# Phase roundings on either engine, half of the filter tables copied in SBUF, split projections in the first batch, and a new written order

## The chip, the cores and the metric

The kernel runs on one core of a Trainium2 chip. A core has five engines that work at the same time, each through its own instructions in order: TensorE for matmuls (PE; its weight loads are listed apart as PEld), VectorE (DVE), ScalarE (ACT), GpSimd (POOL) and SyncE (SP), which here only starts DMA transfers. POOL starts DMA transfers too. They meet through semaphores. Matmuls write PSUM, which has eight banks; DVE and ACT read PSUM, POOL in this kernel works on SBUF alone.

The metric is the device time of one execution in microseconds (us), the median of the runs shown. A "span" is the time from the first to the last instruction of the one profiled execution.

## The reference

Eight batches. First an attention with a feature map in place of a softmax over the sequence, then a gate with a long convolution done by Fourier transforms along the sequence:

```python
def phi(x):
    proj = np.einsum('bhsd,df->bhsf', x, w_phi)
    proj = proj - np.max(np.abs(proj), axis=-1, keepdims=True)
    return np.concatenate([np.exp(proj), np.exp(-proj)], axis=-1)
q_p, k_p = (phi(q), phi(k))
kv = np.einsum('bhsf,bhsd->bhfd', k_p, v)
z = np.sum(k_p, axis=2)
num = np.einsum('bhsf,bhfd->bhsd', q_p, kv)
den = np.einsum('bhsf,bhf->bhs', q_p, z)[..., None] + 1e-06
x = num / den          # then (B, S, H * D)
proj = x @ w_proj
x1, x2, x3 = (proj[..., :D], proj[..., D:2 * D], proj[..., 2 * D:])
X2 = np.fft.rfft(x2, n=S, axis=1)
H = np.fft.rfft(filter_fft, n=S, axis=0)[None, :, :]
x2_conv = np.fft.irfft(X2 * H, n=S, axis=1)
y = x1 * x2_conv * x3
return (y @ w_out).astype(np.float32)
```

Batch 8, heads 8, sequence S = 576, head dimension 64, 128 features, model width D = 512. Inputs and output are float32; the kernel computes in bf16 with float32 sums.

## The kernel before, in words

**An order written out by hand.** The whole program is one string, `PLAN` (lines 28 to 188), of some 1450 words. A word is the name of a method and its arguments; `@n` gives the first PSUM bank that it uses. `run` (L1036) goes through the words and calls each method once, so every engine gets its instructions in the order of the words that use it. Nothing reorders them afterwards. A word such as `Oe,ACT,3,1` or `Oe,DVE,3,1` names the engine that does the step.

**Per batch**, in the names of the words:

- `load` and `loadh` start the transfer of q, k or v (whole, or half the heads) on POOL's queue, with a cast to bf16. `trh` turns q and k by a DMA transpose on SP's queue; for batch 0 PE does this instead (`pt`), and `pte` copies the result from PSUM (into the tiles `qT`, `kT`).
- `Qn` and `Pk` project on PE; `maxq` and `maxk` take the absolute maxima on DVE (L695). `mhi`, `mlo`, `trm`, `trme` bring q's maxima into rows. `Pq` projects q again and subtracts the maxima, all on PE.
- `ex` takes the exponentials on ACT (L681), 16 per batch with both signs, `exkt` and `exqt` those of the last ninth of the sequence. `em` takes exponentials of k's maxima, and `vs` scales v by them (L742): four calls per batch, one for each sign and half.
- `KV` sums over the sequence on PE, `KVe` copies it out. `NE` multiplies by q's exponentials, `rc` and `xn` (L785, L790) divide; `xn,b,v` gives a quarter of the attention output of batch b. `trx` transposes it by DMA into `xT`, in batch 0 `ptx` on PE with `ptxe`. `NEt`, `rct`, `xnt` do the rest of the sequence.
- `f1`, `f2` (L839, L845) fold the output, `F` transforms it on PE, `Fe` and `Fet` copy it out. `X2` projects in the frequency domain, `Y1` (L878, L883) multiplies by the filter's tables, `m3` (L887) adds. `X1` and `X3` project in time through `proj` (L889): eight matmuls of 256 columns, two directions `d` times four row blocks `kt`. `X1e` copies x1 out and `tm` multiplies it by x3.
- `I` transforms back, `Ie`, `Ip`, `Im`, `ym` put halves and the gate together (in the last batch `J` and `yj`), `O` projects out, `Oe` copies, `st` stores on SP's queue.

**The start, once per run.** The cosine and sine tables (`D`, `Dt`, `inv`) are computed on the chip. POOL writes index patterns (`gen_rows`: tiles `fr` and `nr`), DVE writes columns of factors (`gen_cols`: `cols`). A phase is a pattern times a factor; it is rounded to a whole number by writing it as int16 (tile `whole`, L444 and L449) and the remainder (tile `turn`, L438) is what the Sin on ACT takes (`gen_sin`, L459). Both steps stand in `gen_angles` (L433) on DVE. There are nine roundings: two each in `gen_angles,0` and `gen_angles,2`, two in `gen_angles,3` and three in `gen_angles,4`. `D1m` and `D1e` build a mirrored table of `D`. `filt_load` brings the filter in eight transfers on SP's queue, `filt_loadt` its rest; `filt_fold` (L511) adds and subtracts its halves, `H` transforms it on PE, and `H_ev` (L538, L540) writes the tables `HTe`, `HTo` and `H5` from PSUM, with scale factors that are numbers or columns 16 to 18 of `cols`. It reads PSUM nine times.

**The `port` rule.** `run` calls `port` (L1022) after each word. For words in the list `PORT`, when done by DVE, it remembers the DVE instruction; the next POOL step of that list (or a pattern step) gets a dependence on it. So POOL is held until that DVE step is done; there is no such hold the other way.

**Buffers** are rings of tiles (`RING`, `at`), two to six deep; `late` closes the scratch tiles of the start and opens those of the gate.

Of the kernel before, what the change touches and what calls it, by code (L numbers as in the profile page):

```python
# [24 lines left out]
PORT = ("f1", "f2", "m3", "vs", "ym", "mlo", "filt_fold", "gen_ends", "gen_five")  # L25
# [4 lines left out]
gen_part w_load,phi gen_rows,1 gen_cols,0 loadh,q,0,1 filt_load,3 gen_ident gen_cols,1 filt_load,1  # L30
loadh,q,0,0 gen_rows,0 filt_loadt loadh,k,0,0 gen_angles,4 loadh,k,0,1 filt_load,2 load,q,1
w_load,proj,0 pt,q,0,0,0@0 pt,q,0,0,1@1 gen_one gen_sin,4 w_phi filt_load,0 gen_angles,2
w_load,proj,1 load,v,0 gen_angles,3 gen_sin,2 load,k,1 pt,k,0,1,0@2 pt,q,0,1,1@3 gen_angles,0
pt,q,0,1,0@4 gen_neg pt,k,0,1,1@5 pt,k,0,0,1@6 gen_sin,3 pte,DVE,q,0,0,1@1 gen_back gen_sin,0
pte,DVE,q,0,0,0@0 pte,DVE,q,0,1,1@3 Qn,0,0@0 filt_fold,POOL,2 pte,DVE,k,0,1,0@2 pte,ACT,k,0,1,1@5
pt,k,0,0,0@7 trh,q,1,0 pte,DVE,q,0,1,0@4 D1m@2 pte,ACT,k,0,0,1@6 maxq,0,0@0 Qn,0,1@4
pte,ACT,k,0,0,0@7 filt_fold,POOL,1 D1e,ACT@2 Pk,0,1@6 maxq,0,1@4 Pkt,0@0 Qnt,0@2 maxqt,0@2 Pk,0,2@4
trh,q,1,1 filt_fold,POOL,0 maxkt,0@0 ex,k,p,0,2@4 Qn,0,3@2 maxq,0,3@2 exkt,p,0@0 exkt,m,0@0
maxk,0,1@6 ex,k,m,0,2@4 Pk,0,0@2 Qn,0,2@0 load,q,2 ex,k,p,0,0@2 maxq,0,2@0 ex,k,m,0,0@2 maxk,0,2@4
Pk,0,3@0 mhi,0 ex,k,p,0,3@0 zeros H,0@4 maxk,0,0@2 mlo,POOL,0 gen_five,POOL ex,k,m,0,3@0 trm,0@5  # L40
ex,k,m,0,1@6 H,2@2 maxk,0,3@0 H,3@3 ex,k,p,0,1@6 trme,DVE,0@5 H_ev,DVE,0@4 Pq,0,2@0 trh,k,1,0
em,p,0,0 em,m,0,0 H,1@7 vs,POOL,p,0,0 em,p,0,1 H_ev,ACT,3@3 H_ev,DVE,2@2 Pq,0,1@4 H_ev,DVE,1@7 H,4@6
ex,q,p,0,2@0 vs,POOL,m,0,0 ex,q,m,0,2@0 Qn,1,1@2 late trh,k,1,1 H_ev,DVE,4@6 em,m,0,1 ex,q,m,0,1@4
Pq,0,0@0 maxq,1,1@2 Qn,1,0@6 ex,q,p,0,1@4 vs,POOL,m,0,1 maxq,1,0@6 Qnt,1@2 ex,q,m,0,0@0 KV,0,0@4
maxqt,1@2 ex,q,p,0,0@0 vs,POOL,p,0,1 Qn,1,2@6 Pqt,0@2 maxq,1,2@6 KVe,ACT,0,0@4 Qn,1,3@0 trh,q,2,0
exqt,p,0@2 NE,0,0@4 exqt,m,0@2 maxq,1,3@0 Pq,0,3@6 gen_ends,POOL KV,0,1@2 ex,q,m,0,3@6 trh,q,2,1
rc,0,0@4 xn,0,0@4 NE,0,1@0 mhi,1 w_load,out KVe,ACT,0,1@2 mlo,DVE,1 ptx,0,0@4 rc,0,1@0 load,v,1
NE,0,2@2 ptxe,ACT,0,0@4 xn,0,1@0 ex,q,p,0,3@6 rc,0,2@2 f1,POOL,0,0,0 Pkt,1@0 xn,0,2@2 NEt,0@4
maxkt,1@0 NE,0,3@6 f1,POOL,0,0,1 rct,0@4 ptx,0,2@2 exkt,p,1@0 ptx,0,1@3 rc,0,3@6 xn,0,3@6 exkt,m,1@0
f2,POOL,0,0,0 xnt,0,0@4 ptxe,ACT,0,1@3 ptx,0,3@6 ptxe,DVE,0,2@2 trm,1@7 Pk,1,1@0 xnt,0,1@4  # L50
ptxe,ACT,0,3@6 Pk,1,0@2 f1,POOL,0,1,1 maxk,1,1@0 trme,ACT,1@7 ptxt,0@4 ex,k,p,1,0@2 Qn,2,0@5
X1,0,0@7 w_load,proj,2 f1,DVE,0,1,0 ex,k,m,1,0@2 ptxte,DVE,0@4 maxq,2,0@5 f2,POOL,0,1,1 X1,0,2@4
ex,k,m,1,1@0 maxk,1,0@2 f2,POOL,0,1,0 X1t,0@5 X1e,ACT,0,0@7 ex,k,p,1,1@0 Qn,2,2@6 X1te,DVE,0@5
f2,POOL,0,0,1 F,0,2@2 maxq,2,2@6 X1e,ACT,0,2@4 Qn,2,3@0 em,m,1,0 load,k,3 Fet,ACT,0,2@2 F,0,3@4
Fe,ACT,0,2@2 maxq,2,3@0 F,0,0@6 load,k,2 Fet,ACT,0,3@4 Fe,ACT,0,3@4 Qn,2,1@2 Fe,ACT,0,0@6
vs,POOL,m,1,0 Pk,1,3@0 maxq,2,1@2 Qnt,2@4 Fet,ACT,0,0@6 ex,k,m,1,3@0 F,0,1@6 maxqt,2@4 X1,0,1@2
ex,k,p,1,3@0 Fe,DVE,0,1@6 load,q,3 Pq,1,0@4 Fet,DVE,0,1@6 em,p,1,0 maxk,1,3@0 X1e,ACT,0,1@2 Pk,1,2@6
vs,POOL,p,1,0 ex,q,m,1,0@4 X2,0,3@3 maxk,1,2@6 X2,0,2@0 ex,q,p,1,0@4 trh,k,3,1 X2,0,1@1 Y1,0,3@3
em,p,1,1 em,m,1,1 vs,POOL,p,1,1 ex,k,p,1,2@6 X2,0,0@4 Y1,0,2@0 ex,k,m,1,2@6 Pq,1,1@2 Y1,0,0@4
X2,0,4@5 ex,q,m,1,1@2 vs,POOL,m,1,1 trh,k,2,0 KV,1,0@6 mhi,2 Y1,0,4@5 ex,q,p,1,1@2 Y1,0,1@1 Pq,1,2@4  # L60
# [18 lines left out]
trx,2,1 Pqt,2@4 Pq,2,3@6 KVe,ACT,2,1@0 trh,q,4,0 NE,2,0@2 exqt,m,2@4 X2,1,0@0 exqt,p,2@4 rc,2,0@2
xn,2,0@2 ex,q,m,2,3@6 Pq,2,2@4 Y1,1,0@0 f1,POOL,2,0,1 X2,1,1@3 ex,q,p,2,2@4 X2,1,3@2 f1,POOL,2,0,0  # L80
ex,q,m,2,2@4 Y1,1,1@3 trh,q,4,1 X3t,1@0 ex,q,p,2,3@6 f2,POOL,2,0,1 X2,1,4@1 Y1,1,3@2 trh,k,4,0
X1t,1@3 m3,DVE,1,0 Pk,3,1@6 X1te,ACT,1@3 NE,2,2@4 Y1,1,4@1 trx,2,0 ex,k,m,3,1@6 m3,POOL,1,1 NE,2,3@2
rc,2,2@4 O,0,1@1 xn,2,2@4 ex,k,p,3,1@6 rc,2,3@2 trx,2,2 xn,2,3@2 O,0,2@4 Oe,ACT,0,1@1 tmt,1@0
# [107 lines left out]
class Kernel:  # L191
# [901 lines left out]
```

## Time and profile before

| | |
|---|---|
| three runs | 306.33, 313.06, 305.88 us |
| median | 306.33 us |
| the profiled execution | 307.0 us |
| its span | 305.2 us |
| mean granted TensorE clock in it | 0.982 |
| memory read and written in it | 33.75 MB and 9.44 MB |

How to read what follows. The page gives busy time per engine as a share of the span and of the instructions counted; then strips of 40 equal slices, 7.63 us each, in which a digit is the busy share in tenths (9 is 90% or more) and PEclk the granted clock in tenths. The chain of waits goes back from the last instruction through what released each step. Rows of groups have the line, engine and operation, what is written and read, the count, the busy time and the mean in ns of one, and then the idle time just ahead of them with what ended it. Rows of the timeline begin with the start and the length in us. Ends of neighbouring instructions on one engine overlap a little, so the distance from start to start is some 0.1 us shorter than the length.

### The profile page before, as it was taken

The page shows a single profiled execution, that of the slowest core. Times are in us where ns is not written, and L with a number is a line of the kernel's source. Part 1 is how long each engine was busy: PE and PEld are TensorE (multiplying, and loading weights), DVE is VectorE, ACT ScalarE, POOL GpSimd, SP SyncE. Part 2 cuts the span into 40 slices and gives each one's busy share as a digit, 9 for nine tenths or more (in the row PEclk, how much of TensorE's full clock was granted, in tenths as well). Part 3 has the DMA queues.
Part 4 walks back from the last instruction along what each step waited for, and adds up shares of the span by engine and source line. Part 5 has one row for each costly group of instructions (what it writes and reads, how often), then busy time and mean ns, then how long its engine had stood idle before and what let it go on. Part 6 is the DMA issues. An engine that isn't in the chain of part 4 may idle for free.

```text
span 305.2 us, 10169 instructions
## 1 busy us (share of the span) xinstructions
PE 270.7 (89%) x4259; PEld 198.1 (65%) x4289; DVE 258.9 (85%) x444; ACT 218.3 (72%) x370; POOL 227.4 (74%) x199
## 2 busy tenths in 40 slices
PE   0184898998999989999999999999999999999990
PEld 0162486586777668586767778667677857986750
DVE  8768999987987998989998898988899988776940
ACT  3649979984998869987784988788977596631121
POOL 9662899979994898998995995999669855782200
PEclk9996999999999999999999999999999999999997
DMA  6999979996999969996697548697901660361357
GB/s 121 222 206 173 192 120 186 164 170 93 163 177 146 134 138 184 194 150 128 116 180 111 114 60 128 141 166 131 168 5 21 128 142 2 53 133 33 66 127 155
DMA packets 71902, 39.98 MB, mean 131 GB/s; under 512 B 52208, under 2 KB 66672, under 8 KB 71856
## 3 DMA queue, kind: packets, MB, share of 16 engines
q1 hardware_dynamic: 57040, 23.08, 44.8%
q0 software_dynamic: 14816, 16.25, 34.2%
q8 instruction: 33, 0.54, 0.8%
q14 instruction: 13, 0.11, 0.1%
HBM read 33.75 MB, written 9.44 MB: 141 GB/s over the span
## 4 chain that ended last, share of the span: by engine, by line
PE 74%; DVE 11%; DMA 5%; issue 3%; ACT 3%; POOL 2%; SPq 0%; DVEq 0%; POOLq 0%; ACTq 0%
PE ps L895 16%; PE ps L873 11%; PE ps L1007 9%; PE ps L757 6%; PE ps L948 5%; PE ps L771 5%; DVE mq L695 4%; DMA kn<-in_k_dram 3%; PE ps L653 3%; DVE mk L695 2%; PE ps L904 2%; PE ps L851 2%; PE ps L659 2%; PE ps L619 2%; PE ps L855 2%
## 5 line engine op out<-in xcount | busy, mean ns | idle before, releaser
L895 PE MATMUL ps<-xT,wproj 128*128 128x256 bf16 x512 | 65.1, 273 | 1.2 <-DMA xT<-xn 0.8
L895 PEld LDWEIGHTS <-wproj 128*128 128x128 bf16 x512 | 47.5, 98 | 10.5 <-issue 1.9
L695 DVE TENSOR_REDUCE mq<-ps 128x8 f32<-128x1024 f32 (+1 forms) x40 | 43.8, 1112 | 6.0 <-PE ps L626 3.3
L695 DVE TENSOR_REDUCE mk<-ps 128x8 f32<-128x1024 f32 (+1 forms) x40 | 44.2, 1109 | 1.5 <-ACT Ekm L681 1.0
L839 POOL TENSOR_TENSOR SD<-xn 128x512 bf16<-128x512 bf16 x30 | 34.1, 1153 | 12.4 <-DVE xn L790 8.3
L742 POOL TENSOR_TENSOR vp<-vn,vp 128x1152 bf16<-128x1152 bf16 x16 | 34.4, 2152 | 10.3 <-ACT vp L736 8.9
L742 POOL TENSOR_TENSOR vm<-vn,vm 128x1152 bf16<-128x1152 bf16 x15 | 32.2, 2152 | 8.6 <-DVE T L887 6.3
L681 ACT ACTIVATE Eqm<-ps 128x1024 bf16<-128x1024 f32 x32 | 32.7, 1030 | 6.7 <-PE ps L659 5.7
L996 POOL TENSOR_TENSOR yT<-cv,x1s 128x576 bf16<-128x576 f32 x27 | 34.0, 1279 | 4.5 <-DVE cv L955 3.1
L845 POOL TENSOR_TENSOR xf<-SD 128x512 bf16<-128x512 bf16 x32 | 36.5, 1154 | 1.1
L1007 PE MATMUL ps<-wout,yT 128*128 128x512 bf16 x129 | 33.8, 379 | 1.3 <-issue 0.6
L681 ACT ACTIVATE Ekp<-ps 128x1024 bf16<-128x1024 f32 x32 | 33.1, 1035 | 2.1 <-DVE mk L695 1.9
L681 ACT ACTIVATE Eqp<-ps 128x1024 bf16<-128x1024 f32 x32 | 32.9, 1029 | 2.3 <-PE ps L659 2.2
L681 ACT ACTIVATE Ekm<-ps 128x1024 bf16<-128x1024 f32 x32 | 32.8, 1036 | 2.2 <-PE ps L619 1.4
L873 PE MATMUL ps<-wproj,XF 128*128 128x512 bf16 x116 | 30.0, 379 | 0.7 <-issue 0.2
L284 ACT CAST x1s<-ps 128x512 bf16<-128x512 f32 (+1 forms) x31 | 16.7, 548 | 17.5 <-PE ps L904 12.3
L887 POOL TENSOR_TENSOR T<-T,T 128x1024 bf16<-128x1024 bf16 x10 | 21.2, 2126 | 9.3 <-DVE T L883 8.4
L284 ACT COPY o<-ps 128x512 f32<-128x512 f32 x28 | 16.4, 591 | 12.6 <-PE ps L1007 11.6
L955 DVE TENSOR_TENSOR cv<-es,ps 128x288 f32<-128x288 f32 x56 | 22.4, 446 | 2.1 <-ACT es L952 1.9
L948 PE MATMUL ps<-inv,T 128*128 128x288 bf16 x168 | 23.8, 286 | 0.1
L790 DVE TENSOR_TENSOR xn<-ps,r 128x512 bf16<-128x512 f32 x32 | 22.1, 691 | 1.3
L883 DVE TENSOR_TENSOR T<-ps,HTe 128x1024 bf16<-128x1024 f32 x16 | 19.3, 1220 | 4.4 <-PE ps L873 4.4
(169 smaller groups left out, 654.0 us busy)
## 6 DMA issues: line engine op xcount, KB each, us to landing
out_dram<-o SPq DMA_DIRECT2D x72, 128.0 KB, 2.4
vn<-in_v_dram POOLq DMA_DIRECT2D x8, 576.0 KB, 8.5
qn<-in_q_dram POOLq DMA_DIRECT2D x7, 576.0 KB, 9.0
kn<-in_k_dram POOLq DMA_DIRECT2D x7, 576.0 KB, 6.8
wproj<-in_moe_w_proj_dram POOLq DMA_DIRECT2D x3, 512.0 KB, 13.8
fl<-in_moe_filter_fft_dram SPq DMA_DIRECT2D x8, 128.0 KB, 7.1
qn<-in_q_dram POOLq DMA_DIRECT2D x2, 288.0 KB, 7.2
kn<-in_k_dram POOLq DMA_DIRECT2D x2, 288.0 KB, 9.7
```

The costliest lines, as they stand in the source:

```text
L284: self.nc.scalar.copy(dst, src)
L681: self.nc.scalar.activation(e, p, AF.Exp, bias=0.0, scale=1.0 if g == "p" else -1.0)
L695: self.nc.vector.tensor_reduce(out=out, in_=src, axis=AX.X, op=ALU.max, apply_absolute_value=True)
L742: self.eng(eng).tensor_tensor(out=t[:, :, :, 0:64], in0=self.at("vn", b)[:, 2 * X:2 * X + 2], in1=t[:, :, :, 64:65].to_broadcast([128, 2, ...
L839: self.eng(eng).tensor_tensor(out=o[:, :, 2 * i:2 * i + 2, :], in0=x[:, :, 0:2, :], in1=x[:, :, 2:4, :], op=ALU.subtract if i else ALU.add)
L845: self.eng(eng).tensor_tensor(out=o[:, :, 2 * i:2 * i + 2, :], in0=x[:, :, 0:4:2, :], in1=x[:, :, 1:4:2, :], op=ALU.subtract if i else ALU ...
L873: self.mm(self.pb(0), l, w[:, kt, 512:1024], start=(kt == 0), stop=(kt == 3))
L895: self.mm(o[:, d], w[:, kt, f0 + 128 * m:f0 + 128 * m + 128], y[:, 1, ::-1, ::-1] if d else y[:, 0], start=(kt == 0), stop=(kt == 3))
L948: self.mm(self.pb(e, 0, 288), l, inv[:, 2 * e + i if i < 2 else 4 + e, :], start=(i == 0), stop=(i == 2))
L955: self.nc.vector.tensor_tensor(out=self.at("cv", 4 * b + m)[:, :, odd, :], in0=self.at("es", 4 * b + m).rearrange("p (x t) -> p x t", t=32 ...
L996: self.eng(eng).tensor_tensor(out=self.at("yT", b)[:, m, 0:SEQ], in0=self.at("cv", 4 * b + m).rearrange("p x h t -> p (x h t)"), in1=self. ...
L1007: self.mm(self.pb(0), y[:, kt, 128 * c:128 * c + 128], w[:, kt, :], start=(kt == 0), stop=(kt == 3))
```

## The change

- `gen_angles` is taken apart: the roundings become words of their own, `gen_whole,ACT,i` or `gen_whole,DVE,i`. On ACT a rounding is an Identity with scale and bias. The new order has `gen_whole` 0, 3 and 2 on ACT (six roundings) and 4 on DVE (three). Column 39 of `cols` is new and holds 0.25.
- `H_ev` reads PSUM five times, once per filter transform. The other tables are made from these by `H_cp`, SBUF to SBUF: one step on POOL (`H_cp,POOL,0`), three on DVE for `H_cp,DVE,1`, of which two have a single partition, and one for `H_cp,DVE,3`. Columns 16 to 18 hold other factors for that.
- `proj` takes the list of row blocks. In batch 0 each `X1` and `X3` is two words, `X1a` and `X1b` (`X3a` and `X3b`), with two blocks each and other words between them. For all batches the start flag is now set on the first matmul of the bank alone and the stop flag on the last.
- The helper functions `idle` and `warm`, which no word called, and their tile are gone.
- `PLAN` is replaced from its first word to its last, with other banks. Apart from the words named, the same words are there. 98 steps change their engine, in both directions between ACT, DVE and POOL (`Fe`, `Fet`, `X1e`, `Oe`, `KVe`, `ym`, `m3`, `f1`, `f2` and others). At the start: the halves of q are loaded first, then the patterns and the identity, then half of k, q of batch 1, the other half of k, the third part of `w_proj`, and v of batch 0 behind the POOL fold of the filter; folds 2 and 0 are on DVE; `vs` of batch 0 is half on DVE; the phi cast stands ahead of the second part of `gen_cols`.

```diff
-PORT = ("f1", "f2", "m3", "vs", "ym", "mlo", "filt_fold", "gen_ends", "gen_five")
+PORT = ("f1", "f2", "m3", "vs", "ym", "mlo", "filt_fold", "gen_ends", "gen_five",
+        "gen_whole", "H_cp")
...
-        v.memset(cols[:, 16:18], HS)
-        v.memset(cols[0:1, 16:17], 0.5 * HS)
-        v.memset(cols[0:1, 17:18], 0.0)
-        ts(col(18), col(17), -1.0, 0.0)
+        for i, (x, y) in enumerate(((HS, 0.5 * HS), (1.0, 0.5), (-1.0, 0.0))):
+            v.memset(col(16 + i), x)
+            v.memset(cols[0:1, 16 + i:17 + i], y)
...
+    def gen_whole(self, eng, i):
+        cols = self.at("cols")
         col = lambda i: cols[:, i:i + 1]
...
+        def whole(out, x, k, bias, c):
+            if eng == "ACT":
+                self.nc.scalar.activation(out, x, AF.Identity, bias=col(c) if bias else 0.0,
+                                          scale=col(k))
+            else:
+                self.nc.vector.tensor_scalar(out=out, in0=x, scalar1=col(k), scalar2=bias,
+                                             op0=ALU.mult, op1=ALU.add)
...
         for k in ((3, 4), (5, 6, 7))[i - 3]:
-            v.tensor_scalar(out=self.whole[:, 1 + k], in0=self.nr, scalar1=col(k),
-                            scalar2=col(8 + k), op0=ALU.mult, op1=ALU.add)
             rest(k, 1 + k, 2 + k, self.nr)
...
     def H_ev(self, eng, t):
...
+        e, o = self.at("HTe"), self.at("HTo")
+        dst, c = ((e[:, 1, :], HS), (e[:, 3, :], 16), (o[:, 1, :], HS), (o[:, 0, :], -HS),
+                  (self.at("H5"), HS))[t]
+        self.scaled(eng, dst, self.pb(0), c)
+
+    def H_cp(self, eng, t):
+        e, o = self.at("HTe"), self.at("HTo")
         if t == 0:
-            mul(e[:, 1, :], acc, HS)
-            mul(e[:, 2, :], acc, 16)
+            self.scaled(eng, e[:, 2, :], e[:, 1, :], 17)
         elif t == 1:
-            mul(e[:, 0, :], acc, 18)
-            mul(e[:, 3, :], acc, 17)
-            mul(e[0:1, 1, :], self.pb(0, p1=1), 0.5 * HS)
-        elif t == 2:
-            mul(o[:, 1, :], acc, HS)
-        elif t == 3:
-            mul(o[:, 0, :], acc, -HS)
-            mul(o[:, 2, :], acc, HS)
+            self.scaled(eng, e[:, 0, :], e[:, 3, :], 18)
+            self.scaled(eng, e[0:1, 1, :], e[0:1, 3, :], 1.0, 1)
+            self.scaled(eng, e[0:1, 3, :], e[0:1, 3, :], 0.0, 1)
         else:
-            mul(self.at("H5"), acc, HS)
+            self.scaled(eng, o[:, 2, :], o[:, 0, :], -1.0)
...
-    def proj(self, b, f0, m):
+    def proj(self, b, f0, m, kts=(0, 1, 2, 3)):
...
-            for kt in range(4):
+            for kt in kts:
...
-                        y[:, 1, ::-1, ::-1] if d else y[:, 0], start=(kt == 0),
-                        stop=(kt == 3))
+                        y[:, 1, ::-1, ::-1] if d else y[:, 0], start=(kt == 0 and not d),
+                        stop=(kt == 3 and d == 1))
...
+    def X1a(self, b, m):
+        self.proj(b, 0, m, (0, 1))
+
+    def X1b(self, b, m):
+        self.proj(b, 0, m, (2, 3))
```

The new order from the first word to the first maximum, and in the old one the same stretch:

```
before: gen_part w_load,phi gen_rows,1 gen_cols,0 loadh,q,0,1 filt_load,3 gen_ident gen_cols,1
filt_load,1 loadh,q,0,0 gen_rows,0 filt_loadt loadh,k,0,0 gen_angles,4 loadh,k,0,1 filt_load,2
load,q,1 w_load,proj,0 pt,q,0,0,0@0 pt,q,0,0,1@1 gen_one gen_sin,4 w_phi filt_load,0 gen_angles,2
w_load,proj,1 load,v,0 gen_angles,3 gen_sin,2 load,k,1 ... maxq,0,0@0
after:  gen_part w_load,phi gen_cols,0 loadh,q,0,0 filt_loadt loadh,q,0,1 filt_load,2 gen_rows,0
w_phi gen_cols,1 filt_load,1 gen_rows,1 gen_whole,ACT,0 gen_ident filt_load,0 gen_back
gen_whole,ACT,3 gen_one gen_whole,ACT,2 gen_angles,0 loadh,k,0,1 filt_load,3 load,q,1 gen_angles,3
gen_sin,0 pt,q,0,0,1@0 loadh,k,0,0 filt_fold,DVE,2 gen_sin,3 D1m@2 pt,q,0,0,0@1 gen_angles,2
w_load,proj,2 pte,ACT,q,0,0,1@0 D1e,ACT@2 gen_whole,DVE,4 pte,ACT,q,0,0,0@1 pt,q,0,1,1@2 gen_sin,2
gen_angles,4 Qn,0,0@0 pt,q,0,1,0@3 filt_fold,DVE,0 pt,k,0,1,0@4 pte,ACT,q,0,1,0@3 Qn,0,1@6 maxq,0,0@0
```

More of the change, by code (lines that the diff above doesn't have):

```diff
@@ L31 @@
[L31 to L60, printed above, removed]
@@ L79 @@
[L79 to L83, printed above, removed]
-f1,POOL,2,1,0 NEt,2@2 maxk,3,1@6 trx,2,3 Oe,ACT,0,2@4 I,1,0@0 f2,POOL,2,0,0 rct,2@2 I,1,2@4
@@ new lines @@
+X3a,0,1@7 X1e,ACT,0,1@6 maxkt,1@0 ptxt,0@3 f1,POOL,0,1,1 X3b,0,1@7 maxk,1,0@4 ptxte,ACT,0@3
+X1a,0,3@6 X1e,ACT,0,2@2 X1t,0@3 exkt,p,1@0 w_load,out em,m,1,0 F,0,0@4 X1te,DVE,0@3 exkt,m,1@0
+f2,POOL,0,1,0 tm,0,1@7 Qn,2,1@2 Fet,ACT,0,0@4 X1b,0,3@6 Fe,ACT,0,0@4 maxq,2,1@2 f2,POOL,0,1,1
+Qn,2,3@0 X1e,ACT,0,3@6 F,0,1@4 maxq,2,3@0 Pk,1,3@6 mlo,POOL,1 F,0,2@2 load,q,3 ex,k,m,1,3@6
+Fe,DVE,0,2@2 X1a,0,0@0 vs,POOL,m,1,0 ex,k,p,1,3@6 X1b,0,0@0 Fet,DVE,0,2@2 Fet,DVE,0,1@4 trm,1@1
+Fe,DVE,0,1@4 F,0,3@2 X1e,ACT,0,0@0 maxk,1,3@6 trme,ACT,1@1 Qn,2,2@4 Fet,ACT,0,3@2 Fe,ACT,0,3@2
```

323 lines of the change are left out of this document (176 added, 147 removed).

## Prediction

> **What bounds it.** I read the page first (busy shares, the strips, the chain), then stretches of the span cut where the work changes its kind, then the waits, then the timeline of the start.
>
> ```profile
> span 305.2 us, 10169 instructions
> ...
> PE 270.7 (89%) x4259; PEld 198.1 (65%) x4289; DVE 258.9 (85%) x444; ACT 218.3 (72%) x370; POOL 227.4 (74%) x199
> ...
> PE   0184898998999989999999999999999999999990
> ...
> PEclk9996999999999999999999999999999999999997
> ...
> PE 74%; DVE 11%; DMA 5%; issue 3%; ACT 3%; POOL 2%; SPq 0%; DVEq 0%; POOLq 0%; ACTq 0%
> ```
>
> PE is 89% busy as a mean, but the strip shows two kernels in one: from about a third of the span on PE is full, and nearly all that it lacks lies in the first slices and the last. The chain agrees: 74% PE. The stretches, cut at the first maximum of batch 0 (18.86), at the end of its last attention output (46.43) and at the first matmul of batch 3's key-value product (125.69):
>
> ```profile
> 0.00:18.86 18.86, 4.26 (x41) 3.60 (x42) 12.97 (x62) 8.65 (x16) 15.44 (x32) 1.00 0.97 178
> 18.86:46.43 27.57, 20.80 (x410) 14.35 (x410) 24.78 (x37) 24.37 (x41) 17.24 (x21) 0.88 1.10 169
> 46.43:125.69 79.26, 74.98 (x1206) 54.90 (x1215) 71.59 (x107) 67.75 (x116) 67.27 (x55) 1.00 1.07 158
> 125.69:297.57 171.88, 170.02 (x2606) 125.11 (x2629) 149.60 (x241) 116.44 (x199) 127.43 (x93) 1.00 0.61 107
> 297.57:305.20 7.63, 0.69 (x4) 0.10 (x1) 0.00 (x0) 1.08 (x2) 0.00 (x0) 0.75 0.71 155
> 24.70:31.70 7.00, 4.33 (x24) 2.10 (x25) 5.94 (x9) 7.00 (x12) 2.05 (x8) 0.51 1.25 171
> ```
>
> Columns after the length: PE, PEld, DVE, ACT, POOL busy, then granted clock, DMA share, GB/s. PE's idle time is 14.6 us before 18.86, 6.8 in the second stretch, 4.3 in the third, 1.9 in the fourth, 6.9 in the tail. PE has a fixed stock of matmuls, so a new order is worth what it takes from these five numbers. In the second stretch DVE (24.78 of 27.57) and ACT (24.37) set the pace, not PE; the DMA share is 1.10. In the third PE and DVE stand close together: 74.98 and 71.59 of 79.26. From 125.69 on there is almost nothing left to win.
>
> ```profile
> PE ps L600 <- DMA qn<-in_q_dram: 11.9, 1, 11.9
> PE ps L904 <- issue: 1.5, 1, 1.5
> ```
>
> ```profile
> 7.59 0.51 DVE L575 CAST wphi<-phi 128x128 bf16<-128x128 f32 x1
> 8.82 0.75 POOL L578 DMA_DIRECT2D vn<-in_v_dram  x1
> 18.86 1.23 DVE L695 TENSOR_REDUCE mq<-ps 128x8 f32<-128x1024 f32 x1 [0.71 <-PE ps L626]
> 21.90 1.28 ACT L681 ACT_TABLE_LOAD   x1 [0.96 <-DVE mq L695]
> 23.19 1.02 ACT L681 ACTIVATE Ekp<-ps 128x1024 bf16<-128x1024 f32 x1
> 45.74 0.69 DVE L790 TENSOR_TENSOR xn<-ps,r 128x512 bf16<-128x512 f32 x1
> ```
>
> The one long wait is PE's first, for q. Then a chain q, transpose, first maximum at 18.86, first exponential at 23.19 starts the pipeline.
>
> **Part 1: the start, up to the first maximum.** The two halves of q go out first now and the constants that PE needs follow; no row says when q lands then, but it no longer queues behind the key half and the identity. What DVE must do before its first maximum decides. The durations:
>
> ```profile
> L695 DVE TENSOR_REDUCE mq<-ps 128x8 f32<-128x1024 f32 x32 | 38.7, 1218 | 4.1 <-PE ps L626 3.3 <-ACT D L336 0.5
> L438 DVE SCALAR_TENSOR_TENSOR turn<-nr,cols,whole 128x288 f32<-128x288 f32 x5 | 2.6, 519 | 0.2
> L438 DVE SCALAR_TENSOR_TENSOR turn<-fr,cols,whole 128x576 f32<-128x576 f32 x2 | 1.6, 819 | 0.1
> L449 DVE TENSOR_SCALAR whole<-nr,cols 128x288 int16<-128x288 f32 x5 | 2.2, 439 | 0.0
> L444 DVE TENSOR_SCALAR whole<-fr,cols 128x288 int16<-128x288 f32 x4 | 1.4, 403 | 0.0
> L459 ACT ACTIVATE inv<-turn,cols 128x288 bf16<-128x288 f32 x6 | 3.2, 558 | 4.3 <-DVE turn L438 4.3
> L511 POOL TENSOR_TENSOR fe<-fl 128x1024 bf16<-128x1024 f32 x2 | 4.6, 2343 | 0.1
> L499 SPq DMA_DIRECT2D fl<-in_moe_filter_fft_dram x8: 312/426/590, 2.0 to 7.0; - x8
> ...
> DMA to landing us min/median/max: 4.9/7.1/7.9
> ```
>
> Six of the nine roundings leave DVE: 4 x 0.40 + 2 x 0.44 = 2.5 us. On ACT I take 0.56 each (the Sin of the same width), 3.4 us, between DVE's 0.40 and 0.59 (ACT's 512-wide copy); and the order built from the changed kernel holds a third table load, 1.28. That is 4.7 us more on ACT ahead of its first exponential, and one q copy. ACT was busy 8.65 of the first 18.86, so its spare 10 us cover it; I expect the first exponential near 20. Without that cover each microsecond would be late by itself.
>
> DVE takes one fold of the filter (0 on DVE, and POOL's 1 is made to wait for it). A DVE fold has no row; its bounds are 0.82 (the three-operand 576-wide row) and 2.34 (POOL's), and I take 1.2, the row of a 1024-wide DVE pass. It stands directly ahead of the first maximum, and it needs all eight filter loads: the last goes out near 7.0 and lands 4.9 to 7.9 later, 11.9 to 14.9. At the median 14.1, so the first maximum starts at 14.1 + 1.2 = 15.3 (13.1 to 16.1) where it was 18.86: 3.6 us earlier. PE must have the first Qn by then. Its two q copies stand on ACT behind the six roundings, a table load, four Sins and the four copies of D:
>
> ```profile
> 5.09 0.09 POOL L366 MEMSET fr<- 128x1 f32 x1
> 18.21 0.61 PE L626 MATMUL ps<-wphi,qT 64*128 64x128 bf16 x8
> ...
> L284 ACT COPY kT<-ps 128x512 bf16<-128x512 bf16 x2 | 1.1, 589 | 4.3 <-PE ps L600 4.3
> L336 ACT ACTIVATE D<-ps 128x144 bf16<-128x144 f32 x4 | 0.8, 306 | 0.0
> ```
>
> 3.4 + 1.28 + 2.2 + 1.2 + 1.2 = 9.3 us from when the row patterns `fr` are written, 5.2 before and earlier now: 14.5 at the latest, and the first Qn 0.6 later, 15.1. That fits under 15.3. The phi cast moves ahead of the second column constants, so DVE waits there for phi; that is before the filter lands and costs nothing unless phi is late by more than about 2 us.
>
> **Part 2: the stretch to the last output of batch 0.** I count DVE's instructions between the first maximum and that output in both orders.
>
> ```profile
> L742 DVE TENSOR_TENSOR vm<-vn,vm 128x1152 bf16<-128x1152 bf16 x1 | 1.4, 1364 | 0.0
> L742 POOL TENSOR_TENSOR vp<-vn,vp 128x1152 bf16<-128x1152 bf16 x16 | 34.4, 2152 | 10.3 <-ACT vp L736 8.9 <-DVE vm L742 1.2 <-DMA vn<-in_v_dram 0.2
> L540 DVE TENSOR_SCALAR HTe<-ps,cols 128x512 bf16<-128x512 f32 x3 | 2.2, 745 | 0.5 <-PE ps L529 0.5
> L839 DVE TENSOR_TENSOR SD<-xn 128x512 bf16<-128x512 bf16 x2 | 0.8, 425 | 0.1
> L286 DVE COPY qT<-ps 128x640 bf16<-128x640 bf16 x2 | 1.0, 481 | 0.0
> ```
>
> Added: two scalings of v at 1.36 (2.7) and three transposed-block copies at 0.48 (1.4) that stood before 18.86. Removed: seven filter scalings out of PSUM become four, some 0.7 each (2.15), and three small steps that go to ACT, to POOL or past the end (1.1). New: four scalings SBUF to SBUF, without a row; between 0.2 (a 36-wide step) and 0.745 (the PSUM form) I take 0.425, the nearest bf16 pass over 512, so 1.7. The fifth is on POOL, at most about 1.2, with 10 us of idle POOL around it. Net +2.55: DVE has 24.78 + 2.55 = 27.3 us of work. Its idle time was 2.79; with more work ready at its start I take 1.9 (0 to 2.8). The end falls at 15.3 + 27.3 + 1.9 = 44.5 instead of 46.43: **-1.95 us**. So the copies in SBUF save little on DVE: what they save the v scalings eat up.
>
> The clock: between 24.70 and 31.70 it was 0.51 with PE busy 4.33, so full speed would save 2.1 of PE time. PE does not set the pace there, and the new order is as thin on PE: I take -0.3 (0 to -2.1).
>
> **Part 3: from there to batch 3.** The split projection issues the same eight matmuls (two calls of four), so PE's time is unchanged; a half can run when only two of four transposed blocks are there. In the rest of the projections only a flag changes. PE idles 4.28 us in this stretch, 1.51 of it at one point (L904, nothing that the profile shows). I take 3.2 left: **-1.1**, between -4.3 and +4. Up to the same product of batch 3 the new order holds some 2 us less PE work, which comes later; that moves nothing. Behind it and in the tail: 1.9 and 6.9, unchanged, between -1 and +2, since the new order there keeps PE, the full engine, at the same count.
>
> **Sum.** -1.95 - 0.3 - 1.1 = -3.35. The profiled execution took 307.0 with a span of 305.2, the median run 306.33; so 303.6 for a profiled run and **303.0** for the median. About 2% (6.1 us) is what a measurement of this kernel tells from no change.
>
> **A rule that speaks against it.** All the DVE scalings of v read two SBUF tiles, as POOL's do. The trace has them only one after the other: POOL waited 1.2 us for the DVE one. The order written into the program holds POOL behind DVE, not DVE behind POOL. If DVE had to let a running POOL scaling finish, its first v scaling would lose up to 2.15 us, and the sum would be -1.2. The Trainium skill, SBUF — State Buffer, section on the shared port pair, says just this: a DVE instruction with two SBUF inputs and a GpSimd one that reads SBUF exclude each other for the whole instruction, whichever starts first. By that rule 305.2; no run here shows the case.
>
> **Rivals.**
> 1. *DVE becomes the bound.* By the counted words DVE has 72.6 us between 44.5 and batch 3's product, PE 73.1. My forecast leaves DVE 3.7 us idle there, where it had 79.26 - 71.59 = 7.7. If its waits stay as they were, the stretch is 4.0 longer: 307.0. For it: both engines take turns through eight PSUM banks. Against: PE idled only 4.28.
> 2. *The v load comes late.* This is the rival on the slow side.
>
> ```profile
> DMA to landing us min/median/max: 6.5/8.5/19.0
> ```
>
> The load of v stood third from last in POOL's first batch (8.82). Now it stands behind POOL's fold, which waits for DVE's: 15.3 + 2.3 = 17.6. DVE reaches its first v scaling near 29 (15.3, then eight maxima at 1.2, two half as wide, three copies at 0.48 and two scalings at 0.7) and everything on DVE queues behind it, then ACT and PE. With the median the load is there at 26; with the longest, at 36.6, DVE stands 7.6 us: 310.6. It decides against the change from a landing at 32.3. For it: DMA share 1.10 and 1.25 in these stretches. Against: fewer loads stand ahead of it now.
> 3. *DVE and POOL exclude each other*, as above: 305.2.
> 4. *The waits vanish.* Filter at 11.9 (-2.2), no DVE idle in part 2 (-1.9), PE idle 1.5 in part 3 (-1.7): 297.2; most of it, 298.
>
> **Numbers.** Forecast 303.0, 0.38 (own range 300 to 305); rival 1, 0.20; rival 2, 0.11; rival 3, 0.08; rival 4, 0.23. Faster by over 2% (under 300.2): 0.9 of rival 4 and a tenth of the forecast, 0.25. Slower by over 2% (over 312.5): only rival 2 with a second load late too, 0.05. Within: 0.70. The range leaves out the end of rival 4 below 297 and of rival 2 above 309.
>
> **What would show it.** The first DVE maximum at 13 to 16, the first exponential near 20, the last output of batch 0 at 44 to 45, batch 3's product near 120 (the sum and the 2 us moved) with PE idle near 3 before it. A DVE step on v that waits for DMA is rival 2; DVE over 95% busy with PE waiting on it between 45 and 120 is rival 1. I am wrong if the start gains nothing, or if the new order leaves holes in PE after 125, where I put none.

## The result, and the profile after

| | before | after |
|---|---|---|
| median | 306.26 us (4 runs, 305.88 to 313.06) | 310.61 us (4 runs, 310.32 to 311.65) |
| the profiled execution | 307.0 us, span 305.2 | 310.32 us, span 308.5 |
| ratio after to before | | 1.0152, 95% interval 1.0121 to 1.0183 |

The change makes the kernel 1.5% slower, 4.35 us by the medians; 303.0 was forecast, with a range from 297 to 309. Ratios, here and below, leave out executions that were disturbed, while medians and ranges hold all of them; so a median can lie farther out than its ratio says.

The page of after, in the same parts as that of before:

```profile
span 308.5 us, 10181 instructions
...
PE 276.9 (90%) x4289; PEld 200.2 (65%) x4289; DVE 255.6 (83%) x441; ACT 223.2 (72%) x382; POOL 225.1 (73%) x195
...
PE   0578883999998999999989999999999999999990
...
PEclk9999999699999999999999999999999999999997
...
PE 74%; ACT 7%; DVE 7%; DMA 6%; issue 4%; SPq 0%; ACTq 0%; DVEq 0%
PE ps L901 17%; PE ps L879 12%; PE ps L1025 8%; PE ps L763 6%; PE ps L966 5%; DMA qT<-qn 4%; PE ps L777 4%; PE ps L659 3%; PE ps L857 3%; PE ps L861 3%; PE ps L632 2%; PE ps L625 2%; PE ps L910 2%; PE ps L665 2%; PE ps L1004 2%
```

The strip of PE begins better than before (0578 for 0184), but in the seventh slice a 3 stands, and in the slice behind it the clock falls to 6. The chain has a new member, `DMA qT<-qn`, with 4% of the span. (PE's busy sums cannot be compared between the two kernels: before holds 4259 matmul records to 4289 weight loads, after 4289 to 4289, so some are missing there.)

The stretches, cut at the same events: first maximum (13.78), end of the last attention output of batch 0 (42.67), first matmul of batch 3's key-value product (126.08), the tail from 300.93; then two pieces of the third stretch. Columns as in the prediction.

```profile
0.00:13.78 13.78, 3.48 (x29) 2.51 (x30) 10.76 (x57) 10.37 (x21) 7.97 (x25) 1.00 0.89 178
13.78:42.67 28.89, 23.78 (x432) 16.66 (x429) 26.76 (x40) 26.76 (x42) 19.60 (x23) 1.00 1.24 170
42.67:126.08 83.41, 75.58 (x1187) 54.93 (x1187) 71.98 (x114) 64.62 (x109) 69.03 (x55) 0.96 0.95 146
126.08:300.93 174.85, 173.50 (x2646) 126.05 (x2646) 146.10 (x234) 119.94 (x210) 128.46 (x93) 1.00 0.61 110
300.93:308.50 7.57, 0.58 (x3) 0.09 (x1) 0.00 (x0) 1.48 (x3) 0.00 (x0) 0.77 0.73 157
49.30:54.24 4.94, 0.00 (x0) 0.00 (x0) 0.78 (x1) 0.59 (x1) 3.39 (x4) 0.82 1.13 185
54.24:59.00 4.76, 4.75 (x36) 3.33 (x37) 2.65 (x5) 1.94 (x2) 0.35 (x1) 0.50 1.23 207
```

By 42.67 the new kernel is 46.43 - 42.67 = 3.76 us ahead. The loss lies in the third stretch. (The fourth is longer too, 174.85 for 171.88, but PE stands only 1.35 us in it: it holds 17 more weight loads, 2646 for 2629, work that the new order does later. In e3 below, which has no stop, the rest from batch 3's product on is as long, 182.7 for 182.4.) In the third, PE idles 83.41 - 75.58 = 7.83 us, where it had idled 4.28, and 4.94 of them are one stop in which DVE and ACT stand too. After the stop PE is full but has a granted clock of 0.50: 36 matmul records in 4.76 us, where a run below has 57 in the same stretch.

What PE waited for, from the waits and the timeline of PE:

```profile
PE ps L606 <- DMA qn<-in_q_dram: 6.0, 1, 6.0
PE ps L632 <- DMA qT<-qn: 5.0, 1, 5.0
```

```profile
48.32 0.40 PE L632 MATMUL ps<-wphi,qT 64*128 64x128 bf16 x8
48.66 0.61 PE L901 MATMUL ps<-xT,wproj 128*128 128x256 bf16 x4
54.24 0.61 PE L632 MATMUL ps<-wphi,qT 64*128 64x128 bf16 x8 [4.98 <-DMA qT<-qn]
```

The first wait, for q, has halved (11.9 before). The second is new: the second `Qn` of batch 2 stands at the head of PE's queue and waits for the second half of the DMA transpose of q (`trh,q,2`), and everything behind it on PE, then DVE and ACT, waits with it.

The transposes and the loads near them, from the timeline of SP and POOL, first in before, then in after:

```profile
39.41 2.81 SPq L590 DMA_TRANSPOSE qT<-qn  x2
...
41.74 0.81 POOL L571 DMA_DIRECT2D wout<-in_moe_w_out_dram  x1
42.54 0.75 POOL L578 DMA_DIRECT2D vn<-in_v_dram  x1
```

```profile
38.96 3.61 SPq L596 DMA_TRANSPOSE qT<-qn  x2
...
40.80 0.81 POOL L574 DMA_DIRECT2D wproj<-in_moe_w_proj_dram  x1
41.60 0.75 POOL L584 DMA_DIRECT2D vn<-in_v_dram  x1
```

Both kernels have two halves of a transpose and two loads here, but not in the same order. In narrower windows the halves start at 39.41 and 40.88 in before, and the first load comes behind both, 0.9 us after the second. In after they start at 38.96 and 41.19, and the first load, at 40.80, goes out ahead of the second half.

### The profile page after: what moved, and what is told of

It reads as the page before. It is cut to its first block, busy times and chain, and to the rows that moved or that the text cites. A ratio compares the mean times of both kernels' runs of the same rounds, so it can differ in the third digit from the quotient of the medians.

```text
span 308.5 us, 10181 instructions
## 1 busy us (share of the span) xinstructions
PE 276.9 (90%) x4289; PEld 200.2 (65%) x4289; DVE 255.6 (83%) x441; ACT 223.2 (72%) x382; POOL 225.1 (73%) x195
## 4 chain that ended last, share of the span: by engine, by line
PE 74%; ACT 7%; DVE 7%; DMA 6%; issue 4%; SPq 0%; ACTq 0%; DVEq 0%
PE ps L901 17%; PE ps L879 12%; PE ps L1025 8%; PE ps L763 6%; PE ps L966 5%; DMA qT<-qn 4%; PE ps L777 4%; PE ps L659 3%; PE ps L857 3%; PE ps L861 3%; PE ps L632 2%; PE ps L625 2%; PE ps L910 2%; PE ps L665 2%; PE ps L1004 2%
## 5 line engine op out<-in xcount | busy, mean ns | idle before, releaser
L901 PE MATMUL ps<-xT,wproj 128*128 128x256 bf16 x512 | 66.0, 275 | 0.3 <-DVE xnt L808 0.3
L1014 POOL TENSOR_TENSOR yT<-cv,x1s 128x576 bf16<-128x576 f32 x24 | 30.6, 1285 | 14.1 <-DVE x1s L954 5.3
L748 POOL TENSOR_TENSOR vp<-vn,vp 128x1152 bf16<-128x1152 bf16 x15 | 32.3, 2153 | 10.9 <-ACT vp L742 6.7
L1025 PE MATMUL ps<-wout,yT 128*128 128x512 bf16 x144 | 35.4, 380 | 0.0
L851 POOL TENSOR_TENSOR xf<-SD 128x512 bf16<-128x512 bf16 x30 | 34.2, 1155 | 1.0
L893 POOL TENSOR_TENSOR T<-T,T 128x1024 bf16<-128x1024 bf16 x14 | 29.6, 2123 | 6.2 <-DVE T L889 5.1
L879 PE MATMUL ps<-wproj,XF 128*128 128x512 bf16 x128 | 31.4, 380 | 0.0
L286 ACT COPY o<-ps 128x512 f32<-128x512 f32 x30 | 17.6, 604 | 12.1 <-PE ps L1025 10.5
L954 DVE TENSOR_TENSOR x1s<-ps,x1s 128x512 bf16<-128x512 f32 x32 | 21.5, 681 | 2.7 <-issue 1.7
L286 ACT CAST x1s<-ps 128x512 bf16<-128x512 f32 (+1 forms) x25 | 14.3, 585 | 10.9 <-PE ps L901 7.1
```

The lines of the kernel that those rows point to most:

```text
L286: self.nc.scalar.copy(dst, src)
L748: self.eng(eng).tensor_tensor(out=t[:, :, :, 0:64], in0=self.at("vn", b)[:, 2 * X:2 * X + 2], in1=t[:, :, :, 64:65].to_broadcast([128, 2, ...
L851: self.eng(eng).tensor_tensor(out=o[:, :, 2 * i:2 * i + 2, :], in0=x[:, :, 0:4:2, :], in1=x[:, :, 1:4:2, :], op=ALU.subtract if i else ALU ...
L879: self.mm(self.pb(0), l, w[:, kt, 512:1024], start=(kt == 0), stop=(kt == 3))
L893: self.eng(eng).tensor_tensor(out=Y, in0=Y, in1=self.at(f"T{2 * e + 1}", b), op=ALU.add)
L901: self.mm(o[:, d], w[:, kt, f0 + 128 * m:f0 + 128 * m + 128], y[:, 1, ::-1, ::-1] if d else y[:, 0], start=(kt == 0 and not d), stop=(kt = ...
```

## The experiments

Theory A: the half-transposes of q, once loads run beside them, take as long as the loads, and PE's stop and its half clock follow. Theory B: q of batch 2 itself was loaded too late. A third suspect is v of batch 0 (the prediction's second rival).

### 1. The load of q earlier (e1)

```diff
 load,k,1
+load,q,2
...
-load,q,2
 vs,DVE,m,0,0
```

> The changed kernel with one word moved: the load of batch 2's q goes out right behind batch 1's k, ahead of the first part of w_proj and of POOL's v scaling, some 7 us earlier (21 instead of 28.4). Theory A (the second half-transpose of that q shares the DMA engines with the loads issued at 40.8 and 41.6): the transposes cannot start before about 38.9, because PE reads the old contents of that buffer until then, so nothing changes: 310 to 311, PE's wait for qT near 5 us as before. Theory B (the q load itself was too late): the wait goes, the clock stays at 1.00 between 50 and 60, 302 to 305.

Measured: median 310.18 (302.75 to 315.11, 4 runs; no ratio). In the profiled execution (311.39) the wait for `qT` is still there:

```profile
PE ps L632 <- DMA qT<-qn: 5.2, 1, 5.2
```

So an earlier load of q does not by itself end the wait, against theory B. But one of the four executions took 302.75, in the range of theory B, and has no trace; e1 alone does not settle it. e3 does, since it leaves the load of q where it was.

### 2 and 3. Loads behind the transposes (e2, e3)

e2 moves the second part of the projection weights and v of batch 1, e3 the projection weights alone:

```diff
-w_load,proj,1
 rc,0,3@6
...
 f2,POOL,0,0,1
+w_load,proj,1
```

> The changed kernel with two words moved: the second part of w_proj and v of batch 1 are loaded behind the next POOL fold (about 45) and not at 40.8 and 41.6, so the two half-transposes of batch 2's q have the DMA engines to themselves. Theory A: the second half lands near 43 to 44 instead of 54.2, PE's wait of 5.0 us for qT goes, the clock does not fall to 0.5 behind it (worth some 2.5 us more), 302 to 304.5. Theory B (q load too late, collisions irrelevant): 310 to 311.

> As the last one, but only the part of w_proj is moved behind; v of batch 1 still goes out ahead of the fold, now near 40.8. Theory A: one load of 0.59 MB still runs beside the second half-transpose, so it lands near 46 to 49, in time or nearly (PE wants it at 49.3): 303 to 306. Theory B: 310 to 311.

Measured: e3 has a median of 303.77 (301.88 to 307.70, 6 runs), ratio to before 0.9908 (0.9872 to 0.9944): faster than before, in the range of theory A, and 6.8 us under after, by moving one load. PE has no wait for `qT`, and the stretch of the stop looks like this in the windows of e3:

```profile
49.30:54.24 4.94, 4.70 (x72) 3.57 (x71) 4.94 (x8) 4.20 (x9) 4.67 (x6) 1.00 1.22 204
54.24:59.00 4.76, 4.64 (x57) 2.54 (x55) 4.76 (x6) 4.33 (x8) 4.18 (x2) 1.00 1.31 211
```

In e2 the wait is gone too, but it measured 306.63 (303.76 to 312.56, 10 runs), ratio 0.9983 (0.9948 to 1.0019), above the 302 to 304.5 of theory A. In its profiled execution (310.63) v of batch 0 came late: POOL's first scaling waited 4.33 us for it and began at 29.68, and PE waited 2.0 for the scaled v. So the prediction's second rival does occur, in single executions. That execution is one of the longest of the ten; what holds the others near 306 is open, and so is why moving v of batch 1 as well takes back most of what e3 gains.

How a transpose and a load share the DMA engines, from the DMA view, cut to 46 to 48 us (queue; packets, MB, share of the 16 engines; q1 holds SP's transfers, q0 POOL's). First after, then e3:

```profile
q0 software_dynamic: 300, 0.31, 91.1%
q1 hardware_dynamic: 303, 0.08, 29.1%
```

```profile
q1 hardware_dynamic: 1151, 0.29, 81.2%
q0 software_dynamic: 137, 0.13, 40.0%
```

Where both queues are full they get the same number of packets, 300 and 303 here, 289 and 297 from 50 to 52. A packet of a load is about 1 KB (0.31 MB / 300), one of a transpose about 250 bytes (0.29 MB / 1151). So half a transpose, some 1150 packets, gets 150 a microsecond beside a load and would take 1150 / 150 = 7.7 us (an estimate). In after SP's packets come as 205, 303, 160, 297 and 218 in the five windows from 44 to 54, some 10 us; nearly alone, in e3, they go through in two. The Trainium skill, DMA: Bandwidth & Descriptors, section on queues, rings and completion order, says that each DMA engine takes turns between the queues packet by packet; the equal counts agree with that, if the packets that the profile counts are the page's, which no run shows.

From issue to landing the second half took, in before, after and e3:

```profile
qT<-qn SPq DMA_TRANSPOSE x1, 5.0
```

```profile
qT<-qn SPq DMA_TRANSPOSE x1, 13.0
```

```profile
qT<-qn SPq DMA_TRANSPOSE x1, 7.4
```

The turns do not explain all of it. In e3 the load of v (40.51) is ahead of the second half (41.10) too, but it is alone: SP's queue moved only 33 packets from 42 to 46, while the load of v went through, and then 1151 in two microseconds, in time for PE; in after, too, hardly any moved before 44 (80 from 42 on). What keeps the second half from starting once a load is ahead of it is open.

### 4. The collision made in the kernel before (e4)

```diff
+w_load,out
+load,v,1
 vs,POOL,p,0,1
...
-w_load,out
...
-load,v,1
```

> The kernel before with two words moved the other way: w_out and v of batch 1 are loaded near 38.3, ahead of POOL's last v scaling of batch 0, instead of at 41.7 and 42.5, so that they run beside the half-transposes of batch 2's q issued at 39.4. Theory A: the second half lands at 46 to 50 and PE, which wants it at 47.8 to 51, waits 0 to 3 us; with the clock behind it 306.5 to 311. Theory B, or if such a collision is harmless: 306 to 307.

Measured: 309.12 (308.04 to 309.45, 4 runs), ratio 1.0094 (1.0063 to 1.0125). The loads go out at 38.35 and 39.14, the transposes at 40.29, and SP is held by them for 8.68 us (2.81 before); PE waits 1.9 us for `qT` in two waits, and the granted clock between 50 and 55 is 0.66, where before has 1.00. The wait and the window of e4, then the window of before:

```profile
PE ps L626 <- DMA qT<-qn: 1.9, 2, 1.6
```

```profile
50.00:55.00 5.00, 4.37 (x44) 3.25 (x46) 2.98 (x4) 3.51 (x5) 4.88 (x6) 0.66 0.92 139
```

```profile
50.00:55.00 5.00, 4.58 (x77) 3.49 (x76) 4.98 (x6) 4.82 (x12) 4.99 (x6) 1.00 0.92 125
```

The same collision in the old kernel costs about 3 us, in the range of theory A.

### 5. Only v of batch 0 earlier (e6)

```diff
 w_load,proj,2
+load,v,0
...
 filt_fold,POOL,1
...
-load,v,0
```

> The changed kernel with only v of batch 0 moved ahead of POOL's fold; the projection weights and v of batch 1 stay where they collide with the half-transposes. Theory A (the collision carries the loss, v's landing only the spread): PE still waits 4 to 6 us for the half-transposed q of batch 2, near 50 us, and the time is 308 to 310. Rival V (v's late landing, by its knock-on on POOL and DVE, carries the loss): no such wait over 2 us, time 304 or less.

Measured: 312.81 (308.97 to 317.71, 4 runs), ratio 1.0125 (1.0041 to 1.0210). In the profiled execution, the longest of the four (317.71), v is there in time (POOL's scaling starts at 25.47), and PE waits for `qT` all the same:

```profile
PE ps L633 <- DMA qT<-qn: 13.4, 2, 6.9
```

There the two loads, at 40.49 and 41.29, go out ahead of the second half at 42.45. Since none of the four executions came under 308.97 with v ahead alone, late v does not carry the loss; with e3 and e4, the collision does. The median is above the 308 to 310 of theory A: in that trace the collision is worse than in after.

### 6. Both cured (e5, e12)

e5 is e3 with the move of e6. e12 also swaps: the third part of the projection weights goes where the load of v stood.

> The run with the projection load behind, plus one word moved: the load of v of batch 0 goes out ahead of POOL's fold of the filter (issued near 9.2 us, where it was 16.3). Theory A (in the changed kernel two transfers are badly placed: the projection weights collide with the half-transposes of q, and v of batch 0 lands between 25 and 30 from one execution to the next): v lands before 20, POOL's first scaling of v never waits for a DMA, DVE's two scalings of v stay at 1.35 us each because POOL's has ended by 27, and the spread over the executions shrinks from 5.8 us to about 2. Time 301.5 to 303.5. Rival (the start has no room for 0.59 MB more): the filter tables and the second half of k land later, the first maximum moves from 13.8 to 15 or more, and the time is 304 to 306.

> The two moves that helped together, with one more: the load of projection weights that stood behind k of batch 1 in POOL's first batch changes places with the load of v of batch 0, so that the start carries as many loads as in the changed kernel. Theory A: v has landed long before POOL scales it, no wait for half-transposes near 50 us, and the filter tables land as early as in the changed kernel, so the fold starts near 12.7 where the run with v ahead had 13.5; time 300.5 to 303, faster than the kernel before by 1 to 2%. Rival (the projection weights, now issued behind POOL's fold, delay q of batch 2 or k, or meet the transposes of batch 1): a DMA wait of 1 us or more on PE between 25 and 60, time 303 to 306.

Measured: e5 302.51 (301.69 to 310.28, 4 runs), ratio 0.9867 (0.9824 to 0.9911); e12 304.04 (301.42 to 310.66, 6 runs), ratio 0.9873 (0.9821 to 0.9925). The profiled executions have no wait for `qT` and none of POOL for v. Both are faster than either kernel. e5 lies in the range of theory A; the median of e12 is above its 300.5 to 303 and in the rival's range, though PE has no such DMA wait in its trace. The fold starts at 13.49 in e5 and 13.01 in e12, 12.63 in after; that the earlier load of v costs the filter this much is not shown, because in e8 below, without that move, it starts at 14.33. The spread did not shrink to 2 us, and why is not settled, since only one execution of each kernel has a trace.

### 7. The parts of the change, one by one (e7, e8, e10, e11)

e7 is e3 with the six roundings given back to DVE:

```diff
-gen_whole,ACT,0
+gen_whole,DVE,0
...
-gen_whole,ACT,3
+gen_whole,DVE,3
...
-gen_whole,ACT,2
+gen_whole,DVE,2
```

> The run with the projection load behind, with the six roundings that ACT does given back to DVE, at the same places of the order. DVE is busy from 3.5 to 13.8 us but for about 0.3, so by theory A the roundings (0.36 to 0.4 each) push its fold of the filter and the first maximum from 13.8 to about 16, less what the wait for the phi weights (1.0) takes in; ACT loses 3.2 us of work and one table load of 1.28 but waits for DVE's turns. Time 304.5 to 306.5, 1 to 2.5 us more than with the roundings on ACT. Rival (what ACT carries is what starts the exponentials): the first exponential stays at 18.8 or comes earlier, and the time is 303 to 304.

Measured: 304.10 (302.38 to 308.79, 10 runs), ratio 0.9924 (0.9887 to 0.9962), which cannot be told from e3. In the profile (308.21, one of the two longest of the ten) the first maximum starts at 15.75 for 13.84 and the first exponential at 19.68 for 18.76. By this one trace ACT's help is worth 1.9 us at the first maximum and 0.9 at the first exponential, but the time cannot show it; neither of the two expectations is clearly met.

e8 is e3 with the projections of batch 0 in one go, at the place of the second parts:

```diff
-X1a,0,2@2
...
-X1b,0,2@2
+X1,0,2@2
```

> The run with the projection load behind, with the projections of batch 0 summed in one go: the words for the first parts are taken out, and the eight matmuls stand where the second parts stood. Theory A: the split does not carry the gain; PE waits for transposed blocks a few tenths more, time 303.5 to 305. Rival (the split fills PE while the transposed blocks arrive): PE idles 2 us or more between 44 and 70, time 305.5 to 307.

Measured: 306.60 (305.80 to 311.58, 10 runs), ratio 1.0022 (0.9987 to 1.0058): the intervals of e8 and e3 do not meet. The ratios are 1.1% apart, and the time is the rival's: the split carries much of the gain. From the last output of batch 0 to that of batch 1, windows of e3, then of e8:

```profile
42.73:71.52 28.79, 27.51 (x492) 20.70 (x495) 27.61 (x43) 25.35 (x45) 26.68 (x22) 1.00 0.96 152
```

```profile
43.77:74.22 30.45, 28.14 (x492) 20.76 (x495) 27.85 (x43) 25.51 (x45) 27.12 (x22) 1.00 0.96 151
```

With the same 492 matmul records the stretch is 1.66 us longer; PE idles 2.31 for 1.28. Another 1.04 stood there before it, where the fold of the filter began later in that execution (14.33, 12.70 in e3), and nothing in the edit touches the filter. So not all of the 1.1% need be the split's.

e10 is e12 with the second tables written from PSUM again, on DVE:

```diff
         self.scaled(eng, dst, self.pb(0), c)
+        if t in (0, 1, 3):
+            dst, c = {0: (e[:, 2, :], 16), 1: (e[:, 0, :], 18), 3: (o[:, 2, :], HS)}[t]
+            self.scaled(eng, dst, self.pb(0), c)
...
-        if t == 0:
-            self.scaled(eng, e[:, 2, :], e[:, 1, :], 17)
-        elif t == 1:
-            self.scaled(eng, e[:, 0, :], e[:, 3, :], 18)
+        if t == 1:
...
-        else:
-            self.scaled(eng, o[:, 2, :], o[:, 0, :], -1.0)
...
-        for i, (x, y) in enumerate(((HS, 0.5 * HS), (1.0, 0.5), (-1.0, 0.0))):
+        for i, (x, y) in enumerate(((HS, 0.5 * HS), (1.0, 0.5), (-HS, 0.0))):
```

> The run with the same three loads moved, with the copies in SBUF undone: the even table's second copy, the first table and the odd table's second copy are again scaled out of PSUM on DVE (three passes over 512 of 0.67 to 0.74, in place of two SBUF copies of 0.34 and 0.29 on DVE and one of 1.58 on POOL). Theory A (the copies are worth what they save on DVE, which sets the pace between 14 and 43): DVE has 2.1 - 0.6 = 1.5 us more work there, the last output of batch 0 ends 1 to 1.5 later, time 1 to 1.5 us more than with the copies. Rival (the prediction's view, that they save little): under 0.7 us more.

Measured: 303.87 (302.37 to 308.05, 4 runs), ratio 0.9892 (0.9832 to 0.9953); e12 had 0.9873, so the time does not tell them apart. In the profiles the last output of batch 0 ends at 44.29 for 42.45: 1.8 us, a little over what theory A put there. But only 0.7 of it is DVE's added work, which ends at 33.41 for 32.71 ahead of the next maximum; the rest is a wait for PE, which e12 does not have at this place. PE begins the key-value product at 32.85 there, for 30.83 in e12. The maximum in e10:

```profile
34.51 1.22 DVE L699 TENSOR_REDUCE mq<-ps 128x8 f32<-128x1024 f32 x1 [1.11 <-PE ps L630]
```

e11 is e5 with the two scalings of v on DVE given to POOL:

```diff
-vs,DVE,m,0,0
+vs,POOL,m,0,0
...
-vs,DVE,p,0,0
+vs,POOL,p,0,0
```

> The run with the projection load behind and v ahead, with the two scalings of v of batch 0 that DVE does given to POOL, as in the kernel before (2.15 each on POOL in place of 1.35 on DVE). POOL is idle there from 28.4 to 32.9. If DVE sets the pace of this stretch, as the prediction took it, DVE's 2.7 us come back and the time falls by 1 to 2.5 us. Theory A's rival to that: the key-value product of batch 0 then starts at 32.7 instead of 30.7, since POOL's two take 4.3 us one after the other, and what DVE gains is lost to the wait for that product: 0 to 2 us slower.

Measured: 304.61 (303.61 to 316.28, 10 runs), ratio 0.9940 (0.9913 to 0.9966), slower than e5 by about 2 us, as the rival has it. The key-value product of batch 0 starts at 32.72, as expected, but DVE did not get its 2.7 us back either. The timeline of e11, both engines:

```profile
27.93 4.89 DVE L544 TENSOR_SCALAR HTe<-HTe,cols 128x512 bf16<-128x512 bf16 x1
...
28.40 2.16 POOL L748 TENSOR_TENSOR vm<-vn,vm 128x1152 bf16<-128x1152 bf16 x1
30.52 2.15 POOL L748 TENSOR_TENSOR vp<-vn,vp 128x1152 bf16<-128x1152 bf16 x1
```

The copy of a table in SBUF takes 0.35 us on DVE in e5. Here it ends at 27.93 + 4.89 = 32.82, just after POOL's second scaling (30.52 + 2.15 = 32.67): DVE stood for as long as POOL worked.

## Why the prediction was wrong

**The step that failed** is in Part 3: "PE idles 4.28 us in this stretch ... I take 3.2 left: -1.1". It came to 7.83, of which 4.94 is the wait for the transposed q, a wait that the prediction put at nothing without reading a row for it. The growth, 3.55, lies inside the bounds given there (up to +4). What no term held is the half clock behind the stop, 4.76 us at 0.50, some 2.4 us of work at full speed (an estimate); the prediction's clock term looked only at the thin stretch from 24.70. By e3 the collision is worth 6.8 us of the medians: 303.77 without it, beside a forecast of 303.0. That this is so near is in part luck: in e3 the last output of batch 0 comes at 42.73, 1.8 earlier than forecast, but PE still idles 4.1 in the third stretch (3.2 taken), and the rest from batch 3's product on is 3.2 longer than before (2 taken). That rival 2 had priced itself at 310.6, the measured median, is chance: its cause was another.

The prediction looked at one late load (rival 2, v of batch 0) and at the DMA share of 1.10 to 1.25, but not at the one kind of DMA on PE's path whose row it never read: the half-transposes, and which loads are queued beside them. In the words of the order nothing shows it, since `w_load` and `load,v,1` follow `trh,q,2` in both kernels. What could have been priced is the margin, which stands in the DMA view of before, 42 to 44 us:

```profile
q0 software_dynamic: 3, 0.00, 7.1%
q1 hardware_dynamic: 1248, 0.31, 81.0%
```

The last 1248 packets of SP's queue went through there with 3 packets of a load beside them, so loads a microsecond or two sooner run into them. No row was read for that, and it belonged among the rivals on the slow side.

**Part 1, the start: right in kind, its gain too small.** The first maximum was put at 15.3 (13.1 to 16.1) and came at 13.78; the fold cost 1.22 (1.2), the roundings on ACT 0.57 and 0.62 (0.56), the third table load 1.28. Mis-sized is the landing of the filter: the fold started at 12.63, not 14.1, and followed DVE's own work without a wait. The first exponential came at 18.75 ("near 20"). The roundings were taken to be hidden on ACT; they were, but by e7 the time shows little of what they free on DVE.

**Part 2: the count held.** From the first maximum to the last output 27.3 + 1.9 = 29.2 was forecast, and 28.89 measured (DVE busy 26.76, idle 2.13). The end, 44.5 forecast, came at 42.67, so this term was -3.76 instead of -1.95, most of the difference the earlier start. The copies in SBUF took, from the groups of after:

```profile
L544 DVE TENSOR_SCALAR HTe<-HTe,cols 128x512 bf16<-128x512 bf16 x1 | 0.3, 341 | 0.0
L544 DVE TENSOR_SCALAR HTo<-HTo 128x512 bf16<-128x512 bf16 x1 | 0.3, 293 | 0.0
L544 POOL TENSOR_SCALAR HTe<-HTe,cols 128x512 bf16<-128x512 bf16 x1 | 1.6, 1576 | 0.0
```

0.34 and 0.29 where 0.425 was taken; POOL's 1.58 was over the bound of 1.2 and hidden. The view that "the copies in SBUF save little on DVE" put them too low for this stretch, by the traces: e10 ends it 1.8 us later without them, though the times do not tell e10 from e12. The clock term (-0.3) is not shown: after has 1.00 in this stretch for 0.88, but e3, with the same order up to 40 us, has 0.88 again at the same length of 28.89 us.

**The rest of Part 3.** Behind 126.08 and in the tail PE idles 1.35 and 6.99 (1.9 and 6.9 taken as unchanged): right. "The split projection ... PE's time is unchanged" misses that the split keeps PE fed there; without it (e8) the time of the new order, even with the collision gone, cannot be told from that of before. Batch 3's product was put at 120 and came at 126.08; with the collision gone it starts at 120.16 in e3 and 117.70 in e5.

**The rivals.** DVE as the bound (1) did not come: DVE idles 11.4 us of the third stretch. Late v (2) cost POOL a wait of 1.06 in after and 4.33 in e2, but e6 shows that it is not the cause. DVE and POOL excluding each other (3) is real: in after DVE's first scaling took 1.83 instead of 1.35, because POOL's ran until 28.44, a loss of 0.5 where up to 2.15 was allowed. The Trainium skill, SBUF — State Buffer, section on the shared port pair, says that the later of the two waits for the whole instruction; the 1.83 agrees with that: 0.63 until 28.44 and 1.20 behind it. e11 goes further, since there DVE began before the first of POOL's two scalings and stood through both. Of the waits that rival 4 drops, only the one for the filter went; DVE still idled 2.13 in part 2.

**Not tried:** a third buffer for the transposed q, which might let its transposes go out earlier, and the same transposes on PE.

## What to carry to other kernels

When an order changes, list for each DMA that an engine waits for which transfers will be queued beside it, and how much later it may land; here the small transfer with the small packets lost. A load that nobody needs soon is best issued behind such a transfer, even if its queue is free earlier: here one moved word took the change from 1.5% slower to 0.9% faster than before. A gain at the start can be lost if it brings other loads ahead of a transfer that did not move with it.

## What was not expected of the hardware

- Two DMA queues that are both full got equal numbers of packets (300 and 303 in 2 us), so a transpose in packets of about 250 bytes moved 0.08 MB while the load moved 0.31, and about a quarter of the packets that it got in the same time with the other queue nearly empty (303 for 1151 and 1248).
- After a stop of 4.94 us PE's granted clock was 0.50 for the next 4.76 us, though PE was busy in all of them.
- A table copy of 0.35 us on DVE, with one tile in SBUF and a column of factors as its inputs, took 4.89 us beside work on POOL. When the copy began, POOL was issuing a transfer (27.58, 0.80 us), and the first scaling followed 0.02 us later, so the copy probably met no gap; that the issue of a transfer holds DVE too was not tried by itself.
